# Clustered attention with a gated feed-forward block: GpSimd's row sums and weight additions in halves, and one weight chunk rounded in SBUF

## The chip, the cores and the metric

One core of one Trainium2 chip. The metric is device time in microseconds (us). The names of the engines in the profile: PE is TensorE (matrix products; PEld its loading of weights), DVE is VectorE, ACT is ScalarE, POOL is GpSimd, SP issues transfers. Each has its own queue of instructions, which it works off in order; semaphores tie the queues together. A "turn" below is one pass of the kernel's main loop, `t`.

## What is computed

Attention in which a query sees only the keys of its own cluster, and then a feed-forward block over all heads:

```python
def _attn_ref(q, k, v, centroids):          # q, k, v: (4, 8, 768, 64); centroids: (8, 16, 64)
    ...                                     # q_n, k_n, c_n: normalised
    q_assign = np.argmax(np.einsum('bhsd,hcd->bhsc', q_n, c_n), axis=-1)
    k_assign = np.argmax(np.einsum('bhsd,hcd->bhsc', k_n, c_n), axis=-1)
    mask = q_assign[:, :, :, None] == k_assign[:, :, None, :]
    scores = scale * np.matmul(q, k.transpose(0, 1, 3, 2))
    scores = np.where(mask, scores, -1000000000.0)
    ...                                     # attn: softmax of scores
    return np.matmul(attn, v).astype(np.float32)

def _moe_ref(x, w_in, w_out):               # x: (3072, 512); w_in: (512, 2048); w_out: (2048, 512)
    h = x @ w_in
    g = h * (1.0 / (1.0 + np.exp(-1.702 * h)))
    return (g @ w_out).astype(np.float32)
```

q, k, v and the centroids come as float32, the two weight matrices as 64-bit numbers (double precision).

## The kernel before

Three parts matter here.

*Rounding the weights.* A chunk of 128 x 512 weights is loaded as pairs of 32-bit words, and VectorE puts a float32 together from them by integer operations: `a` has sign, exponent and the high bits of the fraction, `e` the low bits, scaled. The last step adds the two. There are 32 chunks (16 of `w_in`, 16 of `w_out`). `engine` makes the addition; `in_psum` says whether `a` stands in a PSUM bank (tile `m` in the profile) or at once in the place of the finished weights (`w_in`, `w_out`) in SBUF. The function is a generator: each `next` emits one step, so that steps can be strewn among other work.

```python
    def rounding(in_psum, engine):
        i = w_done[0]
        load_w(i + 2)
        raw, w = w_raw.pop(i), w_chunks[i][0]
        e = wp.tile([P, WN], I32, name="e", bufs=2)
        a = bank() if in_psum else w
        hi, lo, a_i = raw[:, :, 1], raw.bitcast(U32)[:, :, 0], a.bitcast(I32)
        nc.vector.tensor_scalar(out=a_i, in0=hi, scalar1=3, scalar2=0x3FFFFFF8,   # L174
                                op0=ALU.logical_shift_left, op1=ALU.bitwise_and)
        yield
        nc.vector.scalar_tensor_tensor(out=a_i, in0=hi, scalar=ODD, in1=a_i,      # L178
                                       op0=ALU.bitwise_and, op1=ALU.bitwise_or)
        yield
        nc.vector.tensor_scalar(out=e, in0=a_i, scalar1=POWER, scalar2=None,      # L181
                                op0=ALU.bitwise_and)
        yield
        e = e.bitcast(FP32)
        nc.vector.scalar_tensor_tensor(out=e, in0=lo, scalar=2.0 ** -52, in1=e,   # L185
                                       op0=ALU.mult, op1=ALU.mult)
        engine.tensor_tensor(out=w, in0=a, in1=e, op=ALU.add)                     # L187
        ...                                  # check_w: two operations of ScalarE
        w_done[0] += 1
        yield

    def step(*how):
        if not now and w_done[0] < NW:
            now.append(rounding(*(how or (False, nc.gpsimd))))
        ...                                  # next(now[0])
```

`round_next(...)` emits a whole chunk; `step()` without arguments, called by `advance`, emits one step of a chunk that stands in SBUF and whose addition GpSimd makes.

*The row sums.* The unnormalised attention `A` of a block of 128 keys is 128 x 2 heads x 384 queries. GpSimd adds the six blocks of a group, five additions; TensorE then sums over the partitions (L486), and VectorE takes the reciprocal (L489) and multiplies (L491).

```python
    def mask(u):
        g, kt = divmod(u, NJ)                # group, block of keys in it
        ...
        A = A_of[u]
        if kt == 0:
            return
        if kt == 1:
            sum_of[g] = ap.tile([P, 2, HALF], FP32, name="sum", bufs=2)
        nc.gpsimd.tensor_tensor(out=sum_of[g],                                    # L463
                                in0=A_of[u - 1] if kt == 1 else sum_of[g],
                                in1=A, op=ALU.add)
```

*The main loop.* Each of 96 turns makes two blocks. Eight chunks are rounded whole at chosen turns, by VectorE alone; from turn 14 on, the other 24 go step by step between the other work.

```python
    pace = {t: 1 for t in (0, 2, 5, 8, 9, 11, 12, 13)}
    ...
    for t in range(NT + 2):
        ...                                  # scores(u), part(u), exps(u) of two blocks
        if t > TB // 2 + 1:                  # TB // 2 is 12
            steps[0] += 8
        late = t <= 2 or t == TB // 2 + 1
        if pace.get(t) and not late:
            round_next(True, nc.vector)
        advance(2)
        ...
        for u in us:
            mask(u)
        ...                                  # values of the turn before, preparation, feed-forward
        if pace.get(t) and late:
            round_next(t > 2, nc.vector)
```

`bank()` takes the next of three PSUM banks that go round among rounding in PSUM, the transposed inputs (L295), the nearest centroids (L309, L320), the sums over partitions (L486) and the feed-forward products (L547, L520). `gelu` (ScalarE L510, VectorE L511) reads such a bank. Scores are L417, their exponentials L442, attention times values L474; from turn 24 on a mask is multiplied in by VectorE (L453).

Of the kernel before, what the change touches and what calls it, by code (L numbers as in the profile page):

```python
# [14 lines left out]
ALU = mybir.AluOpType  # L15
# [23 lines left out]
def fast(  # L39
# [26 lines left out]
    nc = tc.nc  # L66
# [8 lines left out]
    HP = H // 2  # L75
# [31 lines left out]
    def bank():  # L107
        return ps_m.tile([P, 512], FP32, name="m")
# [33 lines left out]
    WN = 512  # L142
# [6 lines left out]
    NW = len(w_chunks)  # L149
    w_raw, w_pow = {}, {}  # L150

    def load_w(i):
        if i < NW:
            t = wp.tile([P, WN, 2], I32, name="raw")
            nc.sync.dma_start(out=t.rearrange("p n t -> p (n t)"),
                              in_=w_chunks[i][1])
            w_raw[i] = t
# [5 lines left out]
    w_done = [0]  # L163
# [11 lines that stand above are left out]
                                op0=ALU.logical_shift_left,  # L175
                                op1=ALU.bitwise_and)
# [7 lines that stand above are left out]
        e = e.bitcast(FP32)  # L184
        nc.vector.scalar_tensor_tensor(out=e, in0=lo, scalar=2.0 ** -52, in1=e,  # L185
                                       op0=ALU.mult, op1=ALU.mult)
        engine.tensor_tensor(out=w, in0=a, in1=e, op=ALU.add)  # L187

        check_w(i, raw, w_chunks[NW - 1][0] if i < NW - 1 else raw.bitcast(
            FP32)[:, :, 1])  # L190
        w_done[0] += 1
        yield
# [3 lines left out]
# [4 lines that stand above are left out]
        if now:  # L200
            n = w_done[0]
            next(now[0])
            if w_done[0] > n:
                now.clear()

    def round_next(*how):
        n = w_done[0]
        while w_done[0] == n < NW:
            step(*how)

    def check_w(i, raw, z):

        nc.scalar.activation(out=z, in_=raw.bitcast(FP32)[:, :, 1],
                             func=AF.Square,
                             accum_out=row_sums[:, 2, i:i + 1])
        nc.scalar.activation(out=z, in_=z, func=AF.Exp, scale=-2.0 ** 12,
                             bias=fifteen[:, 0:1],  # L220
                             accum_out=row_sums[:, 3, i:i + 1])
# [55 lines left out]
    for a in range(2):  # L277
        rows = slice(a * D, (a + 1) * D)
        nc.vector.tensor_copy(
            out=cT[rows, :, a, :],  # L280
# [123 lines left out]
    s_of, A_of, sum_of, o_of, O_of, xT_of = {}, {}, {}, {}, {}, {}  # L404

    def split(g):
        b, r = divmod(g, 2 * HP)
        h, hp = divmod(r, HP)
        return b * HP + hp, h

    def scores(u):
        g, kt = divmod(u, NJ)
        p, h = split(g)
        ps = ps_s.tile([P, 2, 512], FP32, name="s")
        for a in range(2):
            rows = slice(a * D, (a + 1) * D)
            nc.tensor.matmul(out=ps[:, a, 0:HALF],  # L417
                             lhsT=T[p, 1][rows, kt * P:(kt + 1) * P],
                             rhs=T[p, 0][rows, h * HALF:(h + 1) * HALF],
                             start=True, stop=(p >= HP))  # L420
        s_of[u] = ps[:, :, 0:HALF]

    def part(u):

        g, kt = divmod(u, NJ)
        p, h = split(g)
        if p >= HP:
            return
        for a in range(2):
            r = 32 * (2 * (p % 2) + a)  # L430
            nc.tensor.matmul(
                out=s_of[u][:, a, :],
                lhsT=hots[p // 2, 1][r:r + NC, kt * P:(kt + 1) * P],
                rhs=hots[p // 2, 0][r:r + NC, h * HALF:(h + 1) * HALF],
                start=False, stop=True)

    def exps(u):
        p, h = split(u // NJ)
        s = s_of[u]
        if p < HP:  # L440
            A_of[u] = ap.tile([P, 2, HALF], FP32, name="A")
        nc.scalar.activation(out=A_of[u] if p < HP else s, in_=s, func=AF.Exp,  # L442
                             scale=SCALE)

    def mask(u):

        g, kt = divmod(u, NJ)
        p, h = split(g)
        s = s_of.pop(u)
        if p >= HP:  # L450
            A_of[u] = ap.tile([P, 2, HALF], FP32, name="A")
            for a in range(2):
                nc.vector.scalar_tensor_tensor(  # L453
                    out=A_of[u][:, a, :],
                    in0=qcode[p][:, a, h * HALF:(h + 1) * HALF],
                    scalar=code[p][:, kt % NH, 1, kt // NH, a:a + 1],
                    in1=s[:, a, :], op0=ALU.is_equal, op1=ALU.mult)
        A = A_of[u]
        if kt == 0:
            return  # L460
        if kt == 1:
            sum_of[g] = ap.tile([P, 2, HALF], FP32, name="sum", bufs=2)
        nc.gpsimd.tensor_tensor(out=sum_of[g],  # L463
                                in0=A_of[u - 1] if kt == 1 else sum_of[g],
                                in1=A, op=ALU.add)

    def values(u):
        g, kt = divmod(u, NJ)
# [28 lines left out]
    def check(g):  # L497


        rec = recs.pop(g)  # L500
        nc.scalar.activation(out=rec, in_=rec, func=AF.Copy,
                             accum_out=row_sums[:, 0, g:g + 1])
        nc.scalar.activation(out=rec, in_=rec, func=AF.Relu, bias=top[:, 0:1],
                             scale=-2.0 * LIMIT * LIMIT,
                             accum_out=row_sums[:, 1, g:g + 1])
# [25 lines left out]
    def advance(n):  # L531
        while n and steps[0] > 0:
            step()
            steps[0] -= 1
            n -= 1
# [65 lines left out]
    TG = NJ // 2  # L601
# [3 lines left out]
    for p in range(1, NPAIR):  # L605
        b, hp = divmod(p, HP)
        for i in range(2 if p == 1 else 0, len(PREP)):
            if p == 1:
                t = (i - 2) // 2
            elif b == 0:  # L610
                t = (hp - 2) * TG + 1 + i // 2
            else:
                t = b * TB + TG * hp - (7, 7, 6, 6, 4, 3, 2)[i]
# [5 lines left out]
    def prep(p, i):  # L619
        if i == 0 and p:  # L620
            load_v(p)
        PREP[i](p)
        if i in (1, 3) and loads:
            load_qk(*loads.popleft())
# [11 lines left out]
    for t in range(NT + 2):  # L636
        us = range(2 * t, 2 * t + 2) if t < NT else ()
        for u in us:
            scores(u)
        if t == 0:  # L640
            prep(0, 6)
        for u in us:
            part(u)
        for u in us:
            exps(u)
        second_half = t >= TB // 2
        if t > TB // 2 + 1:
            steps[0] += 8
        late = t <= 2 or t == TB // 2 + 1
        if pace.get(t) and not late:  # L650
            round_next(True, nc.vector)
        advance(2)
        if recs:
            check(*recs)
        for u in us:
            mask(u)
        work = sorted(prep_at.get(t, ()), key=lambda w: PREP[w[1]] != prep_near)
        while work and PREP[work[0][1]] == prep_near:
            prep(*work.pop(0))
        if 1 <= t <= NT:  # L660
            for u in range(2 * t - 2, 2 * t):
                values(u)

        kept = NF // 2 if t < NT - 3 else NF // 4
        todo = half_ffn or (ffn if len(ffn) > kept else ())
        if not todo:
            owed = 0.0
        elif half_ffn:
            owed += rate
        else:  # L670
            owed += 0.65 if t < NT - 3 else 1.0
        g = (t - 2) // TG if t >= 2 and (t - 2) % TG == TG - 1 else None
        if g is not None and second_half:
            normalise(g)
        advance(1)
        for p, i in work:
            prep(p, i)
            advance(1)
        if g is not None and not second_half:
            normalise(g)  # L680
        while owed >= 1 and todo:
            todo.popleft()()
            owed -= 1
# [3 lines that stand above are left out]
# [184 lines left out]
    for b in range(1, B):  # L871
# [5 lines left out]
        for n in range(NH):  # L877
            sg = sums_g(n)
            if (b, n) == (B - 1, 1):
# [3 lines left out]
                                        op=ALU.min)  # L883
# [454 lines left out]
```

## Time and profile before

| | |
|---|---|
| time, median of 3 | 1038.93 us (1038.92 to 1039.65) |
| span of the profiled execution | 1035.9 us |
| PE busy | 994.2 us (96%) |
| DVE busy | 686.6 us (66%) |
| ACT busy | 374.0 us (36%) |
| POOL busy | 421.3 us (41%) |
| row sums on GpSimd, 128x768 each | 160, 236.2 + 59.2 us |
| weight additions on GpSimd, 128x512 each | 24, 21.5 + 10.9 us |

Busy shares are averages over stages with different limits, so a change is read in the stage where it acts. The weights are rounded between about 16 and 208 us of the span. The duration of an instruction in the trace runs from its start to its end, including any time in which it stands and waits for something other than a semaphore; so one and the same operation can have several durations, and the least of them is the one to compare with.

### The profile page before, as it was taken

What the parts mean: (1) busy time and instruction counts of PE and PEld (TensorE: products, weight loads), DVE (VectorE), ACT (ScalarE), POOL (GpSimd) and SP (SyncE); (2) the same over time, 40 slices, a digit from 0 to 9 for tenths busy, and PEclk for the clock granted to TensorE, in tenths of its full rate; (3) what the DMA queues carried; (4) which work ended last, traced back from release to release, by engine and by line L of the source; (5) the groups of instructions that cost most, each with busy time, mean ns of one, the idle gap of its engine ahead of it and who ended that gap; (6) DMA issues with size and microseconds to landing.
All of it is one profiled execution on the core that took longest, in us unless ns stands there. A gap on an engine that the chain in (4) does not pass through costs nothing.

```text
span 1035.9 us, 12558 instructions
## 1 busy us (share of the span) xinstructions
PE 994.2 (96%) x4574; PEld 583.1 (56%) x4574; DVE 686.6 (66%) x1055; ACT 374.0 (36%) x761; POOL 421.3 (41%) x304
## 2 busy tenths in 40 slices
PE   7998879899999999999999999999999999999997
PEld 4434434344554444544455355688755788656886
DVE  4699998943677687677777667734377534576431
ACT  4676675432455545554554222200122100222000
POOL 2576565432565556655666667500022000120000
PEclk9999998999999999999999999999999999999999
DMA  8413444310012310221000000000000000000000
GB/s 222 131 61 122 148 132 135 100 46 13 19 31 67 87 41 1 62 69 29 21 1 2 10 1 0 1 21 21 22 0 1 1 21 21 21 0 1 21 22 23
DMA packets 66118, 45.25 MB, mean 44 GB/s; under 512 B 52096, under 2 KB 60032, under 8 KB 66048
## 3 DMA queue, kind: packets, MB, share of 16 engines
q1 hardware_dynamic: 65904, 44.33, 14.6%
q8 instruction: 38, 0.62, 0.2%
q14 instruction: 32, 0.26, 0.1%
q10 hardware_dynamic: 144, 0.03, 0.0%
HBM read 38.04 MB, written 6.31 MB: 43 GB/s over the span
## 4 chain that ended last, share of the span: by engine, by line
PE 80%; DVE 16%; ACT 1%; issue 1%; DMA 0%; SPq 0%; DVEq 0%; ACTq 0%
PE b L835 21%; PE b L778 21%; PE s L417 11%; PE o L474 10%; PE m L520 7%; PE m L577 4%; DVE e L185 3%; DVE w_out L178 2%; DVE short L489 2%; PE m L295 2%; DVE e L181 2%; PE m L486 2%; DVE w_in L178 1%; DVE A L453 1%; PE m L309 1%
## 5 line engine op out<-in xcount | busy, mean ns | idle before, releaser
L463 POOL TENSOR_TENSOR sum<-sum,A 128x768 f32<-128x768 f32 x128 | 236.2, 1845 | 137.7 <-DVE A L453 116.8
L453 DVE SCALAR_TENSOR_TENSOR A<-qb,code,s 128x384 f32<-128x384 uint8 x288 | 157.4, 608 | 87.6 <-ACT s L442 52.5
L417 PE MATMUL s<-T,T 64*128 64x384 f32 x768 | 154.7, 516 | 2.9 <-DVE A L453 0.6
L442 ACT ACTIVATE s<-s 128x768 f32<-128x768 f32 x144 | 109.0, 793 | 103.8 <-PE s L417 91.4
L474 PE MATMUL o<-A,inv 128*64 128x384 f32 x768 | 145.1, 499 | 1.0 <-ACT x L479 1.0
L769 DVE TENSOR_TENSOR G<-b,G 128x384 f32<-128x384 f32 x168 | 93.4, 556 | 48.4 <-PE b L778 41.2
L716 POOL TENSOR_TENSOR W<-w_in 128x256 f32<-128x256 f32 x24 | 17.7, 738 | 261.2 <-PE b L778 259.4
L417 PEld LDWEIGHTS s<-T,T 64*128 64x128 f32 x768 | 66.0, 188 | 76.8 <-issue 36.0
L510 ACT ACTIVATE th<-G 128x384 f32<-128x384 f32 x96 | 50.2, 523 | 163.5 <-DVE G L769 103.1
L769 DVE TENSOR_TENSOR y<-b,y 128x256 f32<-128x256 f32 x54 | 22.1, 423 | 130.0 <-PE b L835 93.8
L778 PE MATMUL b<-x,w_in 128*128 128x384 f32 x288 | 101.3, 487 | 0.0
L474 PEld LDWEIGHTS o<-A,inv 128*64 128x64 f32 x768 | 46.6, 136 | 85.2 <-issue 81.2
L489 DVE RECIPROCAL short<-m 128x384 f32<-128x384 f32 x32 | 81.7, 2552 | 9.3 <-PE m L486 9.2
L463 POOL TENSOR_TENSOR sum<-A 128x768 f32<-128x768 f32 x32 | 59.2, 1849 | 64.7 <-DVE A L453 36.7
L511 DVE SCALAR_TENSOR_TENSOR G<-th,G 128x384 f32<-128x384 f32 x96 | 68.5, 713 | 16.8 <-ACT th L510 14.2
L778 PEld LDWEIGHTS b<-x,w_in 128*128 128x128 f32 x288 | 55.0, 191 | 38.2 <-issue 1.1
L778 PE MATMUL b<-x,W 128*128 128x384 f32 x192 | 70.8, 492 | 0.0
L835 PE MATMUL b<-Z,G 128*128 128x256 f32 x288 | 65.1, 379 | 0.0
L520 PE MATMUL m<-w_out,g 128*128 128x512 f32 x120 | 60.0, 619 | 4.2 <-DVE short L329 3.7
L835 PE MATMUL b<-w_out,G 128*128 128x256 f32 x288 | 63.6, 379 | 0.0
L835 PEld LDWEIGHTS b<-w_out,G 128*128 128x128 f32 x288 | 54.7, 190 | 8.0
L835 PEld LDWEIGHTS b<-Z,G 128*128 128x128 f32 x288 | 54.8, 190 | 7.4
(126 smaller groups left out, 1343.4 us busy)
## 6 DMA issues: line engine op xcount, KB each, us to landing
raw<-in_moe_w_in_dram SPq DMA_DIRECT2D x16, 512.0 KB, 4.5
raw<-in_moe_w_out_dram SPq DMA_DIRECT2D x16, 512.0 KB, 3.6
in<-in_q_dram SPq DMA_DIRECT2D x32, 192.0 KB, 3.7
in<-in_k_dram SPq DMA_DIRECT2D x32, 192.0 KB, 3.0
inv<-in_v_dram SPq DMA_DIRECT2D x16, 384.0 KB, 3.9
out_dram<-y SPq DMA_DIRECT2D x15, 256.0 KB, 2.4
qb<-line SPq DMA_DIRECT2D x12, 192.0 KB, 3.3
out_dram<-y SPq DMA_DIRECT2D x18, 128.0 KB, 1.8
```

The source lines that it names most:

```text
L417: nc.tensor.matmul(out=ps[:, a, 0:HALF], lhsT=T[p, 1][rows, kt * P:(kt + 1) * P], rhs=T[p, 0][rows, h * HALF:(h + 1) * HALF], start=True, ...
L442: nc.scalar.activation(out=A_of[u] if p < HP else s, in_=s, func=AF.Exp, scale=SCALE)
L453: nc.vector.scalar_tensor_tensor(out=A_of[u][:, a, :], in0=qcode[p][:, a, h * HALF:(h + 1) * HALF], scalar=code[p][:, kt % NH, 1, kt // NH ...
L463: nc.gpsimd.tensor_tensor(out=sum_of[g], in0=A_of[u - 1] if kt == 1 else sum_of[g], in1=A, op=ALU.add)
L474: nc.tensor.matmul(out=o_of[g][a * D:(a + 1) * D, 0:HALF], lhsT=v_in[p][:, a, kt, :], rhs=A[:, a, :], start=(kt == 0), stop=(kt == NJ - 1))
L489: nc.vector.reciprocal(out=rec, in_=ps[:, 0:HALF])
L510: nc.scalar.activation(out=t, in_=h, func=AF.Tanh, scale=1.702)
L511: nc.vector.scalar_tensor_tensor(out=g, in0=t, scalar=1.0, in1=h, op0=ALU.add, op1=ALU.mult)
L520: nc.tensor.matmul(out=ps[:, 0:DM], lhsT=g, rhs=w_out[:, f, :], start=(f == 0), stop=(f == NF - 1))
L769: nc.vector.tensor_tensor(out=o, in0=p, in1=a, op=ALU.add)
L778: nc.tensor.matmul(out=ps[:, 0:HALF], lhsT=a[:, c], rhs=x(c), start=(c == 0), stop=(c == 1))
L835: nc.tensor.matmul(out=ps[:, 0:DN], lhsT=a(f // 4)[:, f % 4], rhs=z(f), start=(f == 0), stop=(f == FB - 1))
```

## The change

While weights are still being rounded, each row sum is made as two instructions, one for each head (128 x 384 each), and each weight addition that GpSimd makes as two of 256 columns. VectorE's additions stay whole, and so do the row sums once the last chunk is done. It is meant to make the single GpSimd instruction shorter. Besides, the chunk of turn 5 is no longer rounded in PSUM with VectorE's addition; `round_next()` without arguments rounds it in SBUF with GpSimd's addition, so that it needs no PSUM bank.

```diff
-        engine.tensor_tensor(out=w, in0=a, in1=e, op=ALU.add)
+        for n in (0, WN // 2) if engine is nc.gpsimd else (slice(0, WN),):
+            cols = slice(n, n + WN // 2) if engine is nc.gpsimd else n
+            engine.tensor_tensor(out=w[:, cols], in0=a[:, cols],
+                                 in1=e[:, cols], op=ALU.add)
...
-        nc.gpsimd.tensor_tensor(out=sum_of[g],
-                                in0=A_of[u - 1] if kt == 1 else sum_of[g],
-                                in1=A, op=ALU.add)
+        for a in range(2) if w_done[0] < NW else (slice(0, 2),):
+            nc.gpsimd.tensor_tensor(
+                out=sum_of[g][:, a],
+                in0=(A_of[u - 1] if kt == 1 else sum_of[g])[:, a],
+                in1=A[:, a], op=ALU.add)
...
         if pace.get(t) and not late:
-            round_next(True, nc.vector)
+            round_next(*((True, nc.vector) if t > HP * TG // 2 else ()))
```

`HP * TG // 2` is 6, so of the turns in `pace` only turn 5 is affected. The order of the instructions of PE, ACT and SP stays as it was. On VectorE only turn 5's chunk differs (four operations in SBUF instead of five with PSUM). On GpSimd 43 row sums become 86 halves, and the 24 weight additions and turn 5's become 50 halves.

## The prediction

> **What bounds the kernel now.** I read the table of stages first, cut where the rounding of weights begins to matter and where it ends, then the chain of work that ended last. Columns of the stage lines: the stretch, its length, busy time with instruction count of PE, PEld, DVE, ACT and POOL, then the granted TensorE clock, DMA share and GB/s.
>
> ```profile
> 42.00:86.00 44.00, 40.27 (x245) 16.23 (x241) 38.40 (x43) 32.03 (x71) 32.46 (x17) 1.00 0.24 77
> 86.00:209.50 123.50, 107.53 (x448) 50.33 (x444) 115.67 (x142) 71.71 (x168) 68.12 (x43) 0.93 0.42 129
> 209.50:1035.90 826.40, 811.65 (x3664) 498.54 (x3661) 509.93 (x827) 247.35 (x484) 304.22 (x229) 1.00 0.08 22
> ```
>
> After 209.5 us TensorE is busy 98% of the time at full clock: nothing that VectorE or GpSimd do there is worth much, and the change does not touch it. From 86 to 209.5 VectorE is busy 94%, TensorE stands idle for 16.0 us, and its clock is cut to 0.93, a loss of up to 123.5 x 0.07 = 8.6 us of TensorE speed. From 42 to 86 TensorE idles 3.7 us.
>
> ```profile
> PE 80%; DVE 16%; ACT 1%; issue 1%; DMA 0%; SPq 0%; DVEq 0%; ACTq 0%
> ```
>
> VectorE's 16% of the chain is about 166 us. In order of time the chain is almost all VectorE from 57 to 156 and from 166 to 205 us, and TensorE thereafter. So the target is right: what VectorE saves before 209.5 us lets TensorE arrive earlier at its own full stage, up to the idle and clock loss above.
>
> Next I asked what VectorE does there, by shape. Columns: count, total us, mean ns of one, idle before.
>
> ```profile
> L178 DVE SCALAR_TENSOR_TENSOR w_out<-raw,w_out 128x512 int32<-128x512 int32 x16 | 26.5, 1659 | 0.6
> L178 DVE SCALAR_TENSOR_TENSOR w_in<-raw,w_in 128x512 int32<-128x512 int32 x10 | 15.6, 1562 | 0.3
> L178 DVE SCALAR_TENSOR_TENSOR m<-raw,m 128x512 int32<-128x512 int32 x6 | 4.2, 698 | 0.2
> L185 DVE SCALAR_TENSOR_TENSOR e<-raw,e 128x512 f32<-128x512 uint32 x32 | 31.0, 969 | 1.0
> L181 DVE TENSOR_SCALAR e<-w_out 128x512 int32<-128x512 int32 x16 | 9.6, 603 | 1.2
> L181 DVE TENSOR_SCALAR e<-m 128x512 int32<-128x512 int32 x6 | 4.1, 691 | 0.2
> ```
>
> The same L178 takes 0.70 us when its intermediate `m` is in PSUM, and 1.6 us when it is in SBUF. The surplus is waiting counted as busy time. The timeline of both engines shows for what (start, length, instruction):
>
> ```profile
> 112.14 0.42 DVE L174 TENSOR_SCALAR w_in<-raw 128x512 int32<-128x512 int32 x1
> 112.60 1.65 DVE L178 SCALAR_TENSOR_TENSOR w_in<-raw,w_in 128x512 int32<-128x512 int32 x1
> 114.35 1.84 DVE L181 TENSOR_SCALAR e<-w_in 128x512 int32<-128x512 int32 x1
> 116.22 2.18 DVE L185 SCALAR_TENSOR_TENSOR e<-raw,e 128x512 f32<-128x512 uint32 x1
> ```
>
> ```profile
> 112.30 1.39 POOL L187 TENSOR_TENSOR w_in<-w_in,e 128x512 f32<-128x512 f32 x1 [2.15 <-DVE e L185]
> 113.65 4.20 POOL L463 TENSOR_TENSOR sum<-sum,A 128x768 f32<-128x768 f32 x2
> ```
>
> L178 starts at 112.60, stands until GpSimd's addition ends at 113.69, and then does its 0.69 us. L181 stands until the first row sum ends, L185 until the second does. Each GpSimd operation holds back one VectorE operation, and GpSimd in turn waits for the VectorE operation that got in between.
>
> **What the Trainium skill says.** "SBUF — State Buffer", section "Who interferes with whom": a VectorE instruction in a two-port mode, or with two SBUF inputs while GpSimd reads SBUF, and a GpSimd instruction exclude one another for the whole instruction. The trace agrees: blocked are L178 and L185 with SBUF inputs and L174/L181 from SBUF to SBUF; never blocked are the L178 and L181 of PSUM chunks (698 and 691 ns on average) and L489, L511, L326, which read PSUM. "VectorE: DVE Perf Modes", section "Why PSUM operands drop a tier": a PSUM operand excludes the two-port mode; L174 and L181 take 0.41 to 0.43 us in SBUF when unblocked and 0.69 with PSUM. "TensorE: Matmul & The Clock Gate", section "What's actually happening": after about 3.4 us idle the clock is halved. Here gaps of 2.7 to 4.1 us of TensorE stand next to the cut clock, somewhat shorter than the stated window.
>
> **What the change costs and saves, part by part.**
>
> *The size of the pool.* VectorE's waits up to 209.5 us, as (mean minus unblocked time) x count: L178 16 x (1.659 - 0.692) + 10 x (1.562 - 0.692) = 24.2; L185 32 x (0.969 - 0.69) = 8.9; L181 in SBUF 16 x (0.603 - 0.415) + 10 x (0.707 - 0.415) = 5.9; L174 in SBUF about 3.4. Together 42 us. GpSimd's total work does not shrink, so they cannot all go.
>
> *The price of halves.* An unblocked sum of 768 elements takes 1.80 us, an addition of 512 takes 1.26 (least durations of the two tiles). That is 0.54 us per 256 elements, so 0.18 us fixed. A half sum should then take 0.99 us and a half addition 0.72; the 128x256 row of the later weight sums has 0.72 measured. The instruction order of the changed kernel has 86 half sums for 43 whole ones and 50 half additions for 24 (turn 5's is new on GpSimd). Extra GpSimd time: (43 + 24) x 0.18 = 12 us, plus 1.4 for the new addition, on an engine that idles 55 of 123.5 us in the stage. It is affordable, unless a half waits long for each VectorE operation.
>
> *The stretch from 100.6 to 126.8, laid out again.* I keep the order and let the engines alternate, each operation starting when the other releases (GpSimd releases some 0.13 us before its recorded end, as 113.69 against 113.56 above). Four cases come out:
> - One addition followed by VectorE operations that all exclude it (L174, L178, L181, L185): halves just alternate. L178 starts 0.54 earlier, then L181 waits for the second half. Saved: 0.2 us, from the short pauses that now overlap.
> - One addition with L511 after L178: L511 reads PSUM and runs beside the second half. Saved: 0.5.
> - Two sums behind an addition (the lines above): the four half sums meet L181, L185 and the next chunk's L174 and L178. By the end of the second chunk's L185, at 121.7, the saving is 0.9, and 0.1 of it is given back by 126.8.
> - A sum in front of the reciprocal L489 (102.0 to 108.7): the wait of L178 falls from 1.5 to 0.6, the rest runs beside the 2.55 us reciprocal; the last half then meets L491 and L181. Saved: 0.8.
> Sum over the stretch: 0.8 + 0.5 + 0.8 = 2.1, and about 2.4 over the whole recurring pattern of 29.4 us (102.0 to 131.4), of some 11 us of waits in it: 22%. I apply 22% to the waits after 86 us, 42 - 6 = 36: **8 us**.
>
> *PSUM chunks, 57 to 86 us.* Only L185 is exposed there. Three waits of 1.35 to 1.63 us (starting at 60.05, 64.91, 76.88) lose about 0.8 each, since the next operation, L187 with a PSUM input, passes the second half. That is 2.4 us of VectorE, but TensorE idles only 1.6 us in that time, so **1.5 us**.
>
> *Turn 5.* Five PSUM operations of 0.7 us become four in SBUF, and GpSimd makes the addition. L174, L178 and L181 are now exposed to the two sums of that turn (41.83 and 44.05), so my layout has L185 end at 47.4, no sooner than L187 ends now (47.14). What goes is TensorE's wait for the PSUM bank:
>
> ```profile
> PE m L309 <- DVE w_in L187: 2.1, 1, 2.1
> ```
>
> L309 could start once the copies of T end, at 45.9 instead of 47.18: **1.2 us**. The two sums behind that addition come some 1.5 us later; their product L486 comes at 53.6, so there is slack.
>
> *Sum.* 8 + 1.5 + 1.2 = 10.7 us off VectorE's path. TensorE has 19.7 us of idle time to give from 42 to 209.5, but some falls where it is the bound itself (156.7 to 166), so I pass on 90%, 9.6, and add 1 for a cut of the clock that no longer happens. **Predicted 1038.9 - 10.6 = 1028.3 us.**
>
> **The rivals.** *A: alternation gives all back.* If VectorE meets a held port at every operation, as in the first case, the saving is 0.2 us for each of 24 additions, about 5 us, less what longer sums cost; 1033 to 1038. For it: the waits are a property of total GpSimd time, which grows by 13 us. Against: of VectorE's own 80 us in the stage (115.7 less 36 of waits) some 35 read PSUM (L489, L511, L453, L326, L329). *B: GpSimd becomes late.* A sum that ends late delays L486, and through it L489, or holds an A buffer from ScalarE. For: L489 waits 4.2 us for L486 from 38 to 211, and ScalarE's L442 waited 1.7 us once for a sum. Against: POOL's busy share is 55% in the stage, and each pair of sums has a turn of some 9.8 us. This would make 1036 to 1045. *C: a feedback through the clock.* Four gaps of TensorE precede stretches at half clock; if two of them close, TensorE also gains some 3 us at 156 to 166, where it is the bound: 1020 to 1025.
>
> **Range and chances.** Of my sum the 22% is the least certain: 12% gives 1032, 35% with rival C gives about 1022. I set 1021 to 1036. Two per cent would be 1018.2, or 20.7 us, more than all idle time of TensorE from 42 to 209.5, so faster by over 2% needs the clock to recover as well: 0.06. Slower by over 2% needs GpSimd to become the bound: 0.02. Within 2%: 0.92.
>
> **What would show it right or wrong.** In the changed profile L178 in SBUF should fall from 1.6 us to about 1.1 to 1.3, while L181 stays or rises (it meets the second half); L185 should fall from 0.97 to about 0.8. Half sums should read 1.0 to 1.2 us, half additions 0.75 to 0.85. TensorE should reach its saturated stage near 199, not 209.5 us, and the times after that should be shifted and unchanged. TensorE's wait for L187 near 47 should be gone. I am wrong if L178 falls but L181 and L185 rise by as much (rival A), if waits for a sum stand in front of L489 or L442 (rival B), or if VectorE is faster and TensorE's idle time does not shrink.

## The result, and the profile after

| | before | after |
|---|---|---|
| time, median | 1038.93 us (1036.73 to 1039.65) | 1029.22 us (1028.10 to 1030.39) |
| ratio | | 0.991, 95% interval 0.9889 to 0.9931 |
| DVE busy | 686.6 us | 675.9 us |
| POOL busy | 421.3 us | 444.3 us |

The change takes off 9.7 us, 0.9%. Executions of one and the same kernel lie 2 to 6 us apart here, so below a difference is told as a ratio with its interval, and places in single traces are used for mechanism, not for size.

The table of stages of the changed kernel, cut at 200 us because its weights are ready at 201.5 us instead of 208.4; the line to 209.5 has the old borders:

```profile
42.00:86.00 44.00, 42.38 (x251) 16.89 (x249) 36.90 (x43) 33.55 (x76) 36.72 (x36) 1.00 0.26 77
86.00:200.00 114.00, 102.17 (x416) 48.63 (x416) 105.28 (x137) 67.24 (x157) 83.59 (x82) 0.93 0.47 139
86.00:209.50 123.50, 111.67 (x462) 52.58 (x462) 107.48 (x141) 72.79 (x169) 88.62 (x86) 0.93 0.45 132
200.00:1028.50 828.50, 814.31 (x3685) 499.06 (x3681) 511.17 (x830) 249.65 (x490) 305.90 (x231) 1.00 0.08 22
```

TensorE's idle time from 42 to 209.5 falls from 19.7 us to 1.6 + 11.8 = 13.4, and the trace has 711 matrix products there in place of 689. From 86 to 209.5 GpSimd is busy 89 us instead of 68, and the mean clock stays at 0.93. VectorE's share of the chain that ended last falls from 16% to 9%:

```profile
PE 87%; DVE 9%; ACT 2%; issue 1%; DMA 0%; SPq 0%; DVEq 0%; ACTq 0%
```

The rounding operations by shape (line numbers below L174 to L185 are the same in both; the addition is now L189, the sums L469, the reciprocal L496, gelu's VectorE part L518):

```profile
L185 DVE SCALAR_TENSOR_TENSOR e<-raw,e 128x512 f32<-128x512 uint32 x32 | 29.4, 919 | 1.0
L178 DVE SCALAR_TENSOR_TENSOR w_out<-raw,w_out 128x512 int32<-128x512 int32 x16 | 16.9, 1057 | 0.5
L181 DVE TENSOR_SCALAR e<-w_out 128x512 int32<-128x512 int32 x16 | 12.2, 760 | 1.2
L178 DVE SCALAR_TENSOR_TENSOR w_in<-raw,w_in 128x512 int32<-128x512 int32 x11 | 11.4, 1037 | 0.4
L174 DVE TENSOR_SCALAR w_out<-raw 128x512 int32<-128x512 int32 x16 | 10.7, 668 | 0.0
```

L178 has fallen from 1.56 and 1.66 us to 1.04 and 1.06. L181 and L174 have risen (w_out: from 603 and 566 ns to 760 and 668). By the formula of the prediction, (mean minus unblocked time) x count, VectorE's waits go from 42 to 32 us. The stretch shown in the prediction, four VectorE operations from the L174 of the same chunk on, and GpSimd beside it:

```profile
108.41 0.42 DVE L174 TENSOR_SCALAR w_in<-raw 128x512 int32<-128x512 int32 x1
108.86 1.09 DVE L178 SCALAR_TENSOR_TENSOR w_in<-raw,w_in 128x512 int32<-128x512 int32 x1
110.06 0.76 DVE L181 TENSOR_SCALAR e<-w_in 128x512 int32<-128x512 int32 x1
110.86 1.36 DVE L185 SCALAR_TENSOR_TENSOR e<-raw,e 128x512 f32<-128x512 uint32 x1
```

```profile
108.57 1.98 POOL L189 TENSOR_TENSOR w_in<-w_in,e 128x256 f32<-128x256 f32 x2 [1.09 <-DVE e L185]
110.51 5.11 POOL L469 TENSOR_TENSOR sum<-sum,A 128x384 f32<-128x384 f32 x4
```

The three operations behind this L174, and the four of the next chunk, now each wait a little (next chunk: 1.21, 1.37, 1.03 and 1.10 us) where four waited long, and GpSimd waits in turn: four half sums take 5.11 us where two whole ones took 4.20. From this L174 to the end of the next chunk's L185 it was 9.54 us; now it is 8.63.

### The profile page after: what moved, and what is told of

It reads as the page before. It is cut to its first block, busy times and chain, and to the rows that moved or that the text cites. A ratio compares the mean times of both kernels' runs of the same rounds, so it can differ in the third digit from the quotient of the medians.

```text
span 1028.5 us, 12628 instructions
## 1 busy us (share of the span) xinstructions
PE 993.2 (97%) x4574; PEld 581.5 (57%) x4574; DVE 675.9 (66%) x1054; ACT 373.5 (36%) x761; POOL 444.3 (43%) x373
## 4 chain that ended last, share of the span: by engine, by line
PE 87%; DVE 9%; ACT 2%; issue 1%; DMA 0%; SPq 0%; DVEq 0%; ACTq 0%
PE b L842 21%; PE b L785 21%; PE s L420 12%; PE o L481 11%; PE m L527 8%; PE m L584 5%; PE m L554 3%; PE m L298 2%; PE m L493 2%; DVE e L185 1%; DVE short L496 1%; PE m L312 1%; DVE e L181 1%; ACT A L445 1%; PE m L323 1%
## 5 line engine op out<-in xcount | busy, mean ns | idle before, releaser
L469 POOL TENSOR_TENSOR sum<-sum,A 128x768 f32<-128x768 f32 (+1 forms) x162 | 243.6, 1517 | 128.9 <-DVE A L456 117.6
L496 DVE RECIPROCAL short<-m 128x384 f32<-128x384 f32 x32 | 81.6, 2551 | 10.2 <-PE m L493 9.3
L469 POOL TENSOR_TENSOR sum<-A 128x768 f32<-128x768 f32 (+1 forms) x41 | 62.0, 1521 | 60.7 <-DVE A L456 34.0
L518 DVE SCALAR_TENSOR_TENSOR G<-th,G 128x384 f32<-128x384 f32 x96 | 68.6, 714 | 16.9 <-ACT th L517 14.2
L785 PEld LDWEIGHTS b<-x,w_in 128*128 128x128 f32 x288 | 54.7, 190 | 37.9 <-issue 0.5
L842 PEld LDWEIGHTS b<-Z,G 128*128 128x128 f32 x288 | 54.7, 190 | 7.4
```

What stands on the lines that cost most here:

```text
L469: nc.gpsimd.tensor_tensor(out=sum_of[g][:, a], in0=(A_of[u - 1] if kt == 1 else sum_of[g])[:, a], in1=A[:, a], op=ALU.add)
L496: nc.vector.reciprocal(out=rec, in_=ps[:, 0:HALF])
L518: nc.vector.scalar_tensor_tensor(out=g, in0=t, scalar=1.0, in1=h, op0=ALU.add, op1=ALU.mult)
L785: nc.tensor.matmul(out=ps[:, 0:HALF], lhsT=a[:, c], rhs=x(c), start=(c == 0), stop=(c == 1))
L842: nc.tensor.matmul(out=ps[:, 0:DN], lhsT=a(f // 4)[:, f % 4], rhs=z(f), start=(f == 0), stop=(f == FB - 1))
```

## Experiments

**The parts one by one.** Four kernels, each with some of the three edits.

Sums halved alone:

```diff
-        nc.gpsimd.tensor_tensor(out=sum_of[g], ...)
+        for a in range(2) if w_done[0] < NW else (slice(0, 2),):
+            nc.gpsimd.tensor_tensor(out=sum_of[g][:, a], ...)
```

> Only the row sums are halved; the additions stay whole and turn 5 stays in PSUM. My theory (a shorter GpSimd operation lets VectorE reach operations that read PSUM sooner): the sums hold the port longest and stand in front of the reciprocal and of the PSUM chunks, so they bring most: 6 to 7.5 us, about 1032. Rival (the freed PSUM bank of turn 5 is what counts): under 3 us, 1036 or more. Rival (alternation gives all back): 1038 to 1040.

Measured: 1031.47 us, ratio 0.9937 (0.9924 to 0.995), 6.5 us off. As expected.

Additions halved alone:

```diff
-        engine.tensor_tensor(out=w, in0=a, in1=e, op=ALU.add)
+        for n in (0, WN // 2) if engine is nc.gpsimd else (slice(0, WN),):
+            ...                              # columns n to n + WN // 2
```

> Only GpSimd's weight additions are halved. My theory: 0.2 us for an addition followed by operations that exclude it, 0.5 where an operation that reads PSUM follows; over 24 additions some 2 us passed on, about 1037. Rival (alternation gives all back): 1038 to 1040, as the fixed cost of 24 more instructions is not earned.

Measured: 1031.72 us, ratio 0.9941 (0.9921 to 0.996), 6.1 us off, three times what I expected. The trace shows one thing that I had missed. Here is VectorE in the kernel before, ahead of a reciprocal, and what GpSimd does meanwhile:

```profile
101.09 1.25 DVE L174 TENSOR_SCALAR w_in<-raw 128x512 int32<-128x512 int32 x1
102.38 2.18 DVE L178 SCALAR_TENSOR_TENSOR w_in<-raw,w_in 128x512 int32<-128x512 int32 x1
104.47 2.55 DVE L489 RECIPROCAL short<-m 128x384 f32<-128x384 f32 x1
107.06 0.56 DVE L491 TENSOR_TENSOR x<-x,short 128x384 f32<-128x384 f32 x1
```

```profile
100.79 1.27 POOL L187 TENSOR_TENSOR w_in<-w_in,e 128x512 f32<-128x512 f32 x1 [2.15 <-DVE e L185]
102.02 4.21 POOL L463 TENSOR_TENSOR sum<-sum,A 128x768 f32<-128x768 f32 x2
```

And the same place with additions halved and sums whole:

```profile
99.77 0.71 DVE L174 TENSOR_SCALAR w_in<-raw 128x512 int32<-128x512 int32 x1
100.52 1.10 DVE L178 SCALAR_TENSOR_TENSOR w_in<-raw,w_in 128x512 int32<-128x512 int32 x1
101.54 2.54 DVE L492 RECIPROCAL short<-m 128x384 f32<-128x384 f32 x1
104.12 1.49 DVE L494 TENSOR_TENSOR x<-x,short 128x384 f32<-128x384 f32 x1
```

```profile
99.47 1.59 POOL L189 TENSOR_TENSOR w_in<-w_in,e 128x256 f32<-128x256 f32 x2 [1.09 <-DVE e L185]
101.03 4.16 POOL L466 TENSOR_TENSOR sum<-sum,A 128x768 f32<-128x768 f32 x2
```

Before, L174 waits for the whole addition, so the sum is in front of L178, which loses 1.5 us. With halves L174 gets in after the first, L178 waits only for the second, and the sums, still 1.8 us each, fall on the reciprocal, which reads PSUM and takes no longer than before (2.54 us). From L174's start to the reciprocal's it is 3.38 us before and 1.77 now. The multiplication behind it then gives part of this back: it stands 0.9 us until the second sum ends (L494, 1.49 us instead of 0.56). From L174's start to the end of the chunk's L185 it is 7.59 us before and 6.89 now, so 0.7 us remain. A half does not only shorten the wait for itself; it shifts which VectorE operation the next GpSimd operation meets.

This case is a small part of the 6.1 us. In this trace the last L185 of all ends at 202.86 us instead of 207.03, 4.2 us sooner: 0.7 here, four times about 0.5 where L514 stands behind L178, and the rest in steps of mostly 0.2, some of which are lost again. The steps of 0.2 and 0.5 are those that I had laid out. But 24 additions at 0.2 us alone are 4.8, the "about 5 us" of rival A; my 2 us for the additions was added up too low.

Turn 5 alone:

```diff
-            round_next(True, nc.vector)
+            round_next(*((True, nc.vector) if t > HP * TG // 2 else ()))
```

> Only turn 5's chunk is rounded in SBUF, with a whole addition by GpSimd; all GpSimd operations stay whole. My theory: TensorE's wait of 2.1 us near 47 us goes, 1.2 us in the layout with halves, less with whole sums, as VectorE's three SBUF operations then wait up to 1.7 us each for them: 0 to 1 us, 1038 to 1039. Rival (the bank is what counts): 3 us or more, 1036 or less.

Measured: 1037.12 us, ratio 0.9988 (0.998 to 0.9997): about 1.2 us, slightly over the expected range, and far from the bank rival. Its one trace does not show a gain: the second reciprocal stands at 56.5 us, not at 54.7, and the one near 200 us still comes 1.4 us later than before. What the 1.2 us are stays open.

Both halvings without turn 5:

```diff
+        for a in range(2) if w_done[0] < NW else (slice(0, 2),):              # as above
+        for n in (0, WN // 2) if engine is nc.gpsimd else (slice(0, WN),):    # as above
             round_next(True, nc.vector)                                      # as before
```

> The changed kernel without its turn 5: sums and additions halved, turn 5 in PSUM. My theory: about 1.2 us slower than the changed kernel, 1030.5, and the sum of the two halvings (8.5 us). Rival (the bank): 1035 or more. Rival (chance in the clock's cuts): no relation to the sum of the parts.

Measured: 1028.67 us, ratio 0.9908 (0.9895 to 0.9921). That is no slower than the changed kernel with turn 5 (0.991). The bank rival is out. My 1.2 us for turn 5 does not show, but the two intervals leave some 2.5 us either way, so the times alone do not exclude it. The halvings' 6.5 and 6.1 us make 9.6 together (the ratio of before's 1038.74), not 12.6. The case just shown is cured by either: its 7.59 us are 6.91 with sums halved, 6.89 with additions halved and 6.91 in the changed kernel.

**Where turn 5's gain went.** GpSimd in the kernel with both halvings, and in the changed kernel, from turn 5's rounding on:

```profile
42.24 4.63 POOL L467 TENSOR_TENSOR sum<-sum,A 128x384 f32<-128x384 f32 x4 [2.04 <-ACT A L445]
```

```profile
44.30 1.42 POOL L189 TENSOR_TENSOR w_in<-w_in,e 128x256 f32<-128x256 f32 x2 [4.79 <-DVE e L185]
45.68 3.87 POOL L469 TENSOR_TENSOR sum<-sum,A 128x384 f32<-128x384 f32 x4
49.49 2.08 POOL L469 TENSOR_TENSOR sum<-A 128x384 f32<-128x384 f32 x2
```

GpSimd works in order, and its new addition stands in front of this turn's sums: it idles 4.79 us until L185, and the sums start at 45.7 instead of 42.2. L309 does start earlier (44.7 against 46.8), but the late sums then hold back L335 (1.07 us instead of 0.36) and L344, and the reciprocal waits another 0.9 us for a copy of ScalarE. It comes at 54.07 against 54.34, the next one at 66.00 against 65.94. The changed kernel had also come to turn 5 earlier by 0.7 us, although the two do not differ up to there. The chunk's L174 and the reciprocal, with both halvings and in the changed kernel:

```profile
42.59 0.69 DVE L174 TENSOR_SCALAR m<-raw 128x512 int32<-128x512 int32 x1
54.34 2.56 DVE L494 RECIPROCAL short<-m 128x384 f32<-128x384 f32 x1 [0.49 <-PE m L491]
```

```profile
41.89 0.42 DVE L174 TENSOR_SCALAR w_in<-raw 128x512 int32<-128x512 int32 x1
54.07 2.56 DVE L496 RECIPROCAL short<-m 128x384 f32<-128x384 f32 x1 [0.91 <-ACT qb L392]
```

From one to the other it is 11.75 us with the chunk in PSUM and 12.18 with turn 5 changed. To take GpSimd's addition out of this, VectorE makes it:

```diff
-            round_next(*((True, nc.vector) if t > HP * TG // 2 else ()))
+            round_next(*((True, nc.vector) if t > HP * TG // 2 else (False, nc.vector)))
```

> The changed kernel with turn 5's chunk in SBUF but added by VectorE. It keeps the freed bank and takes away GpSimd's addition in front of that turn's sums. If the sums that come later eat what the bank gives, the reciprocal near 54 us and the end come 0.5 to 1.5 us earlier than in the changed kernel, 1027.5 to 1028.5. If VectorE's exposure to the sums eats it, nothing or a loss: 1029 to 1030.

Measured: 1027.86 us, ratio 0.9901 (0.9885 to 0.9916). In the trace the two reciprocals come at 53.92 and 65.50, 0.2 and 0.5 us sooner than in the changed kernel, although all five of VectorE's operations now wait for sums:

```profile
42.62 1.23 DVE L174 TENSOR_SCALAR w_in<-raw 128x512 int32<-128x512 int32 x1
53.92 2.56 DVE L494 RECIPROCAL short<-m 128x384 f32<-128x384 f32 x1 [0.50 <-PE m L491]
```

That is 11.30 us, the shortest of the three: with VectorE's addition the freed bank brings 0.45 us in these traces. It is one trace of each, and the interval of the time overlaps that of the changed kernel: not settled by the times.

The opposite, all chunks of turns 5 to 12 in SBUF with GpSimd's additions:

```diff
-            round_next(*((True, nc.vector) if t > HP * TG // 2 else ()))
+            round_next()
```

> The changed kernel with the chunks of turns 8, 9, 11 and 12 also rounded in SBUF with GpSimd's halved addition. My theory: VectorE's own work falls by 4 x 1.3 us, but L174, L178 and L181 are exposed to the sums of those turns, and TensorE idles only some 1.6 us between 57 and 86 us: within 1.5 us of the changed kernel, 1028 to 1031. Rival (freeing PSUM banks is what turn 5 is about, and each bank brings more): 1026 or less.

Measured: 1035.61 us, ratio 0.998 (0.997 to 0.999), some 7 us slower than the changed kernel by the ratios: both theories missed. The waits from 42 to 90 us tell why (who waited for whom, us in total, times, longest):

```profile
DVE short L494 <- PE m L491: 8.1, 2, 4.4
...
PE m L491 <- POOL sum L467: 2.9, 2, 2.3
```

The additions push GpSimd's sums back until their product L491 and the reciprocal L494 wait for them. This is the prediction's rival B, made real: between 60 and 80 us VectorE is busy 13.8 us here and 19.4 in the changed kernel, GpSimd 18.9 of 20.

**Shorter still.** Both operations in quarters:

```diff
+        parts = 4 if engine is nc.gpsimd else 1
+        for n in range(parts):
+            cols = slice(n * WN // parts, (n + 1) * WN // parts)
...
+        for a, n in ([(a, n) for a in range(2) for n in range(2)] ...):
```

> The changed kernel with both GpSimd operations cut in four instead of two while weights are rounded (sums 128x192, additions 128x128); same work, twice the instructions. My theory: a quarter sum should take 0.58 us and a quarter addition 0.45 (0.18 fixed plus 0.54 per 256 elements), so VectorE is held for less each time, but the fixed cost adds some 12 us to GpSimd and most VectorE operations alternate: between 2 us faster and 2 us slower than the changed kernel, 1027 to 1031. Rival (the length of one GpSimd operation is all that matters): a further 4 us or more off, 1025 or less. Rival (GpSimd becomes late): 1033 or more, with waits for sums.

Measured: 1029.04 us, ratio 0.9909 (0.9895 to 0.9924), the same as halves. VectorE's waits for GpSimd's operations, by the same formula, shrink further, from 32 to 20 us, but another takes their place. The stage of the quarters, and VectorE's two longest waits for semaphores in it:

```profile
86.00:200.00 114.00, 100.27 (x417) 47.59 (x414) 95.63 (x136) 65.92 (x154) 107.73 (x167) 0.94 0.46 138
```

```profile
DVE e L181 <- POOL w_in L190: 5.7, 3, 3.2
DVE e L181 <- POOL w_out L190: 4.8, 2, 3.2
```

GpSimd is busy 107.7 of 114 us: it is late, and L181 waits for one of the two buffers `e` that GpSimd has still to read. Rival B again.

**How much there is.** Two kernels that leave work out, so their outputs are not the reference's. First, four of five row sums of each group left out while weights are rounded:

```diff
+        if kt > 1 and w_done[0] < NW:
+            return
         nc.gpsimd.tensor_tensor(out=sum_of[g],
```

> The kernel before, leaving out four of the five row sums of each group while weights are rounded (the output's normalisation is then not the reference's). It shows what all exclusion by sums costs. My theory: VectorE loses its waits for sums, about 20 us of 42, and TensorE has 19.9 us of idle time and 8.6 us of cut clock to give: about 1022 to 1026. Rival (VectorE's waits are not on the path): 1034 or more.

Measured: 1023.72 us, ratio 0.9856 (0.9838 to 0.9874), as my theory has it. Second, GpSimd's weight additions left out too:

```diff
+        if engine is nc.vector:
             engine.tensor_tensor(out=w, in0=a, in1=e, op=ALU.add)
```

> As the run without sums, and GpSimd's 24 weight additions are left out too (the weights lose their low bits), so nothing on GpSimd excludes VectorE while weights are rounded. It is the most that any cutting of GpSimd's operations can bring. My theory: VectorE's waits go to nearly nothing, TensorE becomes the bound from 42 us on, and the time falls to about 1014 to 1020; halves then bring about half of what there is to have. Rival (the path is set by other things in the stage): above 1028, no better than the changed kernel.

Measured: 1013.63 us, ratio 0.9763 (0.9746 to 0.978): 24.6 us below the median of before (1038.2, as 1013.63 / 0.9763). The stages:

```profile
42.00:86.00 44.00, 41.92 (x253) 16.79 (x249) 36.42 (x48) 35.02 (x77) 5.44 (x3) 1.00 0.30 89
86.00:200.00 114.00, 111.09 (x489) 53.02 (x488) 87.45 (x147) 73.66 (x171) 12.96 (x7) 1.00 0.48 145
```

With GpSimd out of the way TensorE idles 2.9 us from 86 to 200, and its clock is not cut there. Halves bring 9.7 of these 24.6 us, some 40%.

**Fewer exclusions instead of shorter ones.** L174's result goes to a PSUM bank, L178 reads it there, and its own result goes to SBUF, where GpSimd needs it. On top of the changed kernel:

```diff
+        m_i = a_i if in_psum else bank().bitcast(I32)
-        nc.vector.tensor_scalar(out=a_i, in0=hi, ...)
-        yield
-        nc.vector.scalar_tensor_tensor(out=a_i, in0=hi, scalar=ODD, in1=a_i,
+        nc.vector.tensor_scalar(out=m_i, in0=hi, ...)
+        nc.vector.scalar_tensor_tensor(out=a_i, in0=hi, scalar=ODD, in1=m_i,
...                                          # after L185
+        yield
```

> The changed kernel, but in a chunk whose addition GpSimd makes the result of L174 goes to a PSUM bank and L178 reads it there, in one step; its result goes to SBUF as before. Neither excludes GpSimd then, only L181 and L185 do, and the addition is a step of its own. My theory: VectorE's waits at L174 and L178 (16 us in the changed kernel's trace) go, partly moving to L181 and L185; L174 costs 0.27 us more for each of 25 chunks (7 us); so VectorE gains 3 to 8 us, and the time is 1023 to 1028 if TensorE can spare the bank. Rival (the bank counts): TensorE waits for VectorE at a bank of its own, and the time is 1032 or more.

Measured: **1017.70 us, ratio 0.9817 (0.9795 to 0.9839)**, better than both kernels of this study and than I expected.

```profile
L185 DVE SCALAR_TENSOR_TENSOR e<-raw,e 128x512 f32<-128x512 uint32 x32 | 29.9, 933 | 0.8
L175 DVE TENSOR_SCALAR m<-raw 128x512 int32<-128x512 int32 x32 | 21.9, 685 | 1.2 <-ACT qb L393 1.2
L178 DVE SCALAR_TENSOR_TENSOR w_out<-raw,m 128x512 int32<-128x512 int32 x16 | 11.0, 688 | 0.6
L181 DVE TENSOR_SCALAR e<-w_out 128x512 int32<-128x512 int32 x16 | 8.7, 543 | 1.7
```

```profile
86.00:200.00 114.00, 105.93 (x464) 49.11 (x462) 96.26 (x140) 72.25 (x168) 78.92 (x86) 1.00 0.47 141
```

L174 (here L175) and L178 run unblocked at 0.69 us. Their waits did not move to L181, which falls too, and hardly to L185 (933 ns against 919). And the clock stands at 1.00, which I had not counted on; no gap of TensorE's is longer than 1.8 us. The addition has also become a step of its own, and L174 and L178 share one; what that alone is worth was not separated.

The mirror image, L181's result in PSUM and read there by L185:

```diff
+        e_i = e if in_psum else bank().bitcast(I32)
-        nc.vector.tensor_scalar(out=e, in0=a_i, ...)
-        yield
+        nc.vector.tensor_scalar(out=e_i, in0=a_i, ...)
```

> As the last one, but it is L181's result that goes to a PSUM bank, and L185 reads it there in the same step; L174 and L178 stay exposed. My theory: the waits at L181 and L185 (17 us in the changed kernel's trace) go, partly moving to L174 and L178, for 25 x 0.27 = 7 us: again 1023 to 1028. Rival (the bank counts): 1032 or more.

Measured: 1038.64 us, ratio 1.0007 (0.9999 to 1.0016). VectorE's waits for GpSimd fall to about 12 us here too (11 in the form before), yet all is lost elsewhere:

```profile
86.00:200.00 114.00, 97.74 (x395) 46.78 (x393) 87.41 (x126) 64.02 (x148) 70.33 (x76) 0.90 0.43 134
```

```profile
PE m L300 <- DVE e L185: 5.5, 3, 2.4
...
PE m L556 <- DVE e L185: 2.4, 1, 2.4
```

VectorE is busy only 87 of 114 us, and of the 16.3 us that TensorE idles in this stage it waits 7.9 at PSUM banks that L185 still reads. So the bank rival holds for this form and not for the other, though both take one bank a chunk. The forms differ in the step that takes the bank, and so in the other uses that this falls between; whether that is the reason was not tried.

Last, the better form with whole sums and additions and turn 5 as before:

```diff
+        m_i = a_i if in_psum else bank().bitcast(I32)                        # and the rest, as above
         engine.tensor_tensor(out=w, in0=a, in1=e, op=ALU.add)                # whole, as before
             round_next(True, nc.vector)                                      # as before
```

> The kernel before with only L174's result in a PSUM bank (as in the run at 1017.7 us), whole sums and additions, turn 5 as before. If the time is set by how many operations of VectorE exclude GpSimd, and not by the length of GpSimd's own, the halves bring little here: 1018 to 1020. If the halves remain worth part of their 9.7 us, since L181 and L185 still meet whole sums of 1.8 us: 1021 to 1026. If the two changes simply add: 1027.

Measured: 1029.31 us, ratio 0.9912 (0.9893 to 0.9931). The two changes add: 0.9912 x 0.991 = 0.9823, measured together 0.9817. Of the three outcomes that I had written down this is the last: the halves lose nothing of their worth.

## Why the prediction held, step by step

- *The bound and the target.* Held. The time comes from before 209.5 us: the reciprocals shift by 2.2 us at 80, 4.2 at 104, 6.7 at 199, and stay at 6.8 to 7.4 from there to the last at 583 us. The span of this pair of traces differs by 7.4 us; the medians by 9.7.
- *The price of halves.* Held: the shortest half sum is 0.99 us, the shortest half addition 0.72. On average they take 1.12 and 0.93; the additions are above my 0.75 to 0.85, since two of them with VectorE in between take 1.98 us (at 108.57), and 1.42 without (at 44.30).
- *The layout of the stretch.* Held closely for the long case: 8.63 us against 8.6 laid out (9.54 less 0.9). In front of the reciprocal (from 100.6 to L185's end) 8.05 us became 7.38, laid out 7.25. What the layout gave to the sums there, the additions alone bring as well.
- *The 22%, 8 us after 86 us.* It came out smaller in the traces. The last L185 of the PSUM chunks ends at 85.95 us before and 84.44 after, the last of all at 207.03 and 200.01: 5.5 us in between, and 6.9 with both halvings alone.
- *PSUM chunks.* Held: 1.5 us expected. With both halvings alone the L185 of turn 5 ends 0.4 us sooner than before (46.00 against 46.40), that of the last PSUM chunk 1.9 us sooner (84.09 against 85.95).
- *Turn 5, 1.2 us.* Failed. My layout set L174 to L181 against the sums of that turn; but the addition stands in front of those sums, so VectorE was not exposed at all (L185 ends at 44.2, not 47.4) and the sums came 3.4 us later, not 1.5, onto L335 and L344, which take 0.8 us longer than without. TensorE's wait for L187 is gone, as said (its only wait from 42 to 60 us is the line below the list), but the reciprocal has none of it, and the times do not show it either: 0.991 with turn 5, 0.9908 without. With whole operations about 1.2 us showed, which no trace explains.
- *The sum.* The total of 10.6 us was right in size, in part by luck. The halves alone gave 9.6 (8.2 to 10.9), where I had passed on 8.5 from them, and the other 2.1 did not show: turn 5 gave nothing that the times can tell, and the clock's cuts between 42 and 209.5 us last 17 us in the trace before and in the one after.
- *Signs.* L178 fell more than I wrote (1.05 against 1.1 to 1.3), L181 rose (of w_out; that of w_in stayed), both as said; L185 fell to 0.92 and not to 0.8, since sums meet it where they had met L181: with additions alone halved it is 1.06, with sums alone 0.85.
- *Rivals.* A, that alternation gives all back, is excluded by the halvings' 0.9908. B is not seen in the changed kernel, but in its neighbours (quarters; all chunks in SBUF), so it was closer than I gave it. C, the clock, did not come here, but it did in the form at 1017.70.

TensorE's waits from 42 to 60 us in the changed kernel, where the prediction showed 2.1 us for L187:

```profile
PE m L385 <- DVE hot L344: 0.3, 1, 0.3
```

The statement of the Trainium skill, "SBUF — State Buffer", section "Who interferes with whom", that an instruction with at most one SBUF input outside the two-port modes does not contend, holds in the trace of the form at 1017.70 for the new L178: 27 instructions with `raw` in SBUF and `m` in PSUM, writing SBUF, at 0.69 us on average beside a busy GpSimd.

## What to carry to other kernels

When one operation has two durations in a profile, look at what the neighbouring engine runs at that moment: time that counts as busy may be waiting for that engine, and cutting the other engine's operations in two lets the wait end sooner, until the fixed cost of more instructions makes that engine late. Better still, look for the operand whose move to PSUM takes the instruction out of the exclusion, and count what a bank costs at that very step. An operation moved to an engine that works in order also delays everything behind it: ask what stands there and who reads it.

## What the runs showed of the hardware that I had not expected

- GpSimd's additions of float32 follow one line from 128 to 768 columns: least durations 0.44 us (128), 0.58 (192), 0.72 (256), 0.99 (384), 1.26 (512), 1.80 (768), that is 0.18 us plus 2.1 ns a column.
- A waiting VectorE operation gets in between two GpSimd operations that stand ready one behind the other: that is why halves help at all. In the stretch of the prediction the first sum stands at 113.65 us, L178 ends its 0.69 us at 114.25, and the two sums take 4.20 us instead of 2 x 1.80.
- The length of a gap of TensorE does not settle whether its clock is cut. With L174 in PSUM and whole sums it was cut to half from 48.1 us on, for 3.4 us, after a gap of 2.1 us (44.7 to 46.8); in the kernel before, a gap of the same 2.1 us at the same place (45.1 to 47.2) was followed by no cut. The later cuts of that kernel stand at gaps of 2.7, 2.9, 4.1 and 3.7 us, so only two of the four are shorter than the 3.4 us that the prediction quotes. In the kernel at 1017.70, whose longest gap is 1.8 us, the clock was not cut from 42 to 215 us.
